# Attention and max-of-three feed-forward on one core: when batch 0 prepares its weights, and what the first steps load and wait for

## The chip, the core and the metric

The kernel runs on one core of a Trainium2 chip. The metric is the time of one execution in microseconds (us) on the device. Before the change it was run three times: 772.04, 774.18 and 776.42 us, median 774.18 us. A trace comes from one profiled execution more, of 775.52 us. In this document PE is the matrix engine (PEld its weight loads), DVE the vector engine, ACT the scalar engine, POOL the GpSimd engine, and SP the engine that issues most DMAs.

## The reference, cut to what matters

For 8 batches, 8 heads, 576 positions and head size 64:

```
rel    = i - j                                   (query minus key position)
scores = q k^T / 8 + slope_h * (-|rel|)          where 0 <= rel < 128, else -1e9
attn   = softmax(scores);  x = attn v            -> x is 4608 tokens x 512
h      = max(x w1, x w2, x w3)                   512 -> 768, elementwise maximum
out    = h w_out                                 768 -> 512
```

All in float32. Each query sees itself and at most 127 positions before it, so attention is done in bands of 128 queries.

## The kernel before

**Attention.** A task is one batch and one pair of heads (four tasks a batch). Two tasks give nine steps of 128 queries, so a batch has 18 steps (the name `n_steps`). Each two steps share one set of score matmuls (`products`, L381), then for each step come a masked copy and a fused add, scale and row minimum on DVE (`score`, L396, L399, L410), two exponentials on ACT (`exps`, L422), a reciprocal and the division (`sums_of`, `normalise`, L428 to L441), a transpose on PE with its copies (`turn`, L450 to L474) and the product with v (`mix` or `mix_rows`, L495 and L517).

**Feed-forward.** Products in nearly full float32 are made from two rounded pieces of each operand (hi and lo), and of 2x2 blocks with seven products instead of eight (a Strassen scheme). A weight group is 128 columns of w1, w2 or w3: nine groups, 0 to 8, and groups 9, 10 and 11 are the three parts of w_out. A unit is one of the seven products of one group for one batch: six matmuls of 128 by 288 (L707). A batch has 63 such units, and then 14 units that multiply by w_out.

**Weights.** They are prepared once, during batch 0. `preparing` (L270) is a generator that goes through the groups in the order `g_order` and does one of six parts each time that it is asked: the exponents, the conversion, parts 0 and 1 (round to hi on ACT, lo = source minus hi on DVE), part 2 and part 3 (sums of blocks on PE, then the same split). The first four groups of the order take a form with the exponents on DVE (L156, L165); the other eight have them on ACT (L158, L159, L169). A prepared group 0 to 8 lies in a ring of two places, is stored to DRAM for the later batches (`store`, L192), and its place is free for the group two later when the units that read it are done (`ahead`). If the next part has to wait for that, the generator stands still. The w_out groups have places of their own. The raw weights of a group come by DMA (`fetch`, L145) into one of two buffers.

**Who asks for parts.** `weights(n, upto)` adds n to an account and does one part for each whole one in it, and more if fewer than `upto` are done. Events are written out in order by `at(step, ...)` and sorted. Steps 5 to 19 ask for 1.6 parts each, and every unit of batch 0 for 1.3; in a unit `upto` is such that the parts that this unit multiplies by are done ahead of its matmuls in the program. Batch 0's units lie in the program between the steps of batch 1's attention. From the counters, the order puts these parts into these stretches:

```
parts of 72, in program order        steps 5-19   units 0-20   units 21-56
before (1.6 a step, 1.3 a unit)            25           19            28
groups begun in units 21-56: 5, 6, 7, 8 (each eight or nine units ahead of its first unit)
```

**Order of instructions.** The program order is the priority, and a scheduler at build time lets an engine take a later instruction where an earlier one isn't ready in its own model. An instruction given to `keep_in_program_order` stays where it is relative to its engine's others. Once built, each engine runs its list in order. `spin` (L325) puts bf16 matmuls of zeros on PE: seven at the start, and four after each second step of batch 0.

**The start.** SP issues q and k of task 0 (two DMAs), v of task 0, the identity, the raw weights of group 0, q and k of task 1, the raw weights of group 1, in this order. The score matmuls of steps 4 and 5 need q and k of task 1.

Of the kernel before, what the change touches and what calls it, by code (L numbers as in the profile page):

```python
# [26 lines left out]
RING = 2  # L27
SPIN, FIRST_SPIN = 4, 7

# [5 lines left out]
def attention_maxout_kernel(  # L35
# [117 lines left out]
    def exponents(g, few):  # L153
        _, t, top, small = pieces(g)
        if few:
            nc.vector.tensor_scalar(out=small, in0=top, scalar1=-56.0, scalar2=56.0, op0=ALU.max, op1=ALU.min)  # L156
        else:
            nc.scalar.activation(small, top, AF.Relu, bias=-56.0)  # L158
            nc.scalar.activation(t.bitcast(F32), top, AF.Relu, scale=-2.0 ** 27, bias=-56.0 * 2.0 ** 27)  # L159
# [107 lines left out]

    g_order = [0, 1, 9, 10, 11, 2, 3, 4, 5, 6, 7, 8]

# [93 lines left out]
    def products(s):  # L363
        whole = s < n_steps and s % 4 == 2
        ps = [ps_m.tile([P, 512], F32, name=f"ps_m{j}") for j in range(2)] if whole else [scores[:, j] for j in range(2)]
        for a, (t, i) in enumerate(steps[s:s + 2]):
            banks[s + a] = [x[:, a * 2 * P:(a + 1) * 2 * P] for x in ps], None if whole else a
            for j in range(2):
                for h in range(2):
# [16 lines left out]
                    ))  # L386

    def score(s):
        t, i = steps[s]
        b, hp = tasks[t]  # L390
        ps, a = banks.pop(s)
        if i:
            mask = prev[:, i == NB].bitcast(mybir.dt.uint8)
            if a is None:
                for x in ps:
                    nc.vector.copy_predicated(x[:, P:2 * P], mask, x[:, :P])  # L396
            else:
                both = scores[:, :, a * 2 * P:(a + 1) * 2 * P]
                nc.vector.copy_predicated(  # L399
                    both[:, :, P:], mask.unsqueeze(1).broadcast_to([P, 2, P]), both[:, :, :P],  # L400
                )

# [4 lines left out]
        for j in range(2):  # L407
            x = s_p.tile([P, P], F32, name="s", bufs=3)
            below = bias_t[:, hp // 2, j] if i == NB else (bias if i else bias0)[:, 2 * hp + j, :]
            nc.vector.tensor_tensor_reduce(  # L410
                out=x, in0=ps[j][:, P:2 * P], in1=below,
                scale=-0.125, scalar=3.0e38, op0=ALU.add, op1=ALU.min, accum_out=st[:, 0, s % 2, j:j + 1],
            )
            less[s].append(x)
# [256 lines left out]
    def unit(u):  # L671
# [14 lines left out]
        if g < 9:  # L686
            at = b * 9 + g
            if b == 0:
                weights(1.3, 6 * g_order.index(g) + 3 + (2, 2, 3, 3, 1, 2, 1)[k])
            x = xs[b, k]  # L690
# [86 lines left out]
    for s in range(5, n_steps + 2):  # L777
        at(s + 0.2, weights, 1.6)
        at(s + 0.7, rest)
# [9 lines left out]
    load(0)  # L789
    load_v(0)  # L790
    nc.sync.dma_start(dist[:, 2], c_ident)
    slopes(0)
    slopes_t(0)
    fetch(0)
    nc.scalar.copy(out=plus, in_=dist[:, 2])
    nc.scalar.activation(minus, dist[:, 2], AF.Copy, scale=-1.0)
    load(1)
    fetch(1)
# [40 lines left out]
```

## Time and profile before

| | |
|---|---|
| runs | 772.04, 774.18, 776.42 us |
| profiled execution | 775.52 us |
| its span, first to last instruction | 773.8 us |
| PE busy | 752.0 us (97%), weight loads 683.2 us (88%) |
| DVE, ACT, POOL busy | 546.6 (71%), 519.2 (67%), 193.5 us (25%) |
| mean granted PE clock | 0.991 of full speed |

Busy is the time in which an engine had at least one instruction in work. A row of a stage table gives the stretch, its length, busy time and instruction count (x) for each engine, the granted PE clock (1.00 is 2.4 GHz, 0.50 is 1.2 GHz), the share of the DMA engines and GB/s. A timeline row gives the start, the length, the engine, the line, the operation and its tiles, and in brackets the idle time of the engine just before and what ended it.

### The profile page before, as it was taken

What the parts mean: (1) busy time and instruction counts of PE and PEld (TensorE: products, weight loads), DVE (VectorE), ACT (ScalarE), POOL (GpSimd) and SP (SyncE); (2) the same over time, 40 slices, a digit from 0 to 9 for tenths busy, and PEclk for the clock granted to TensorE, in tenths of its full rate; (3) what the DMA queues carried; (4) which work ended last, traced back from release to release, by engine and by line L of the source; (5) the groups of instructions that cost most, each with busy time, mean ns of one, the idle gap of its engine ahead of it and who ended that gap; (6) DMA issues with size and microseconds to landing.
All of it is one profiled execution on the core that took longest, in us unless ns stands there. A gap on an engine that the chain in (4) does not pass through costs nothing.

```text
span 773.8 us, 19378 instructions
## 1 busy us (share of the span) xinstructions
PE 752.0 (97%) x7243; PEld 683.2 (88%) x7247; DVE 546.6 (71%) x1698; ACT 519.2 (67%) x1680; POOL 193.5 (25%) x403
## 2 busy tenths in 40 slices
PE   7898999999999999999999999999999999999998
PEld 2467787899999999999999999999999999999998
DVE  3878698986667947886677847785677847693673
ACT  5697889967668767677577766676676756652342
POOL 4350212311223222221232122221222122243100
PEclk8998999999999999999999999999999999999999
DMA  6674577783798649883788659983888558789721
GB/s 244 230 263 133 192 288 275 263 277 119 259 315 289 211 146 325 295 287 128 254 299 289 201 174 322 307 274 112 285 300 274 187 196 283 271 262 359 240 71 62
DMA packets 43838, 184.95 MB, mean 239 GB/s; under 512 B 4832, under 2 KB 14304, under 8 KB 34912
## 3 DMA queue, kind: packets, MB, share of 16 engines
q0 software_dynamic: 20304, 115.61, 45.1%
q1 hardware_dynamic: 23296, 67.97, 25.2%
q8 instruction: 57, 0.93, 0.5%
q14 instruction: 37, 0.30, 0.1%
q10 hardware_dynamic: 144, 0.13, 0.1%
HBM read 157.74 MB, written 25.95 MB: 237 GB/s over the span
## 4 chain that ended last, share of the span: by engine, by line
PE 67%; DVE 13%; ACT 7%; issue 1%; DVEq 0%; ACTq 0%
PE ps_m L707 54%; PE ps_s L381 4%; PE ps_x L517 4%; PE pt L450 3%; DVE hs L565 2%; ACT p L422 2%; DVE t L662 2%; DVE hq L663 2%; DVE t L568 1%; ACT t L723 1%; DVE xs L565 1%; PE pt L201 1%; ACT p L441 1%; ACT hs L564 1%; DVE xk L551 1%
## 5 line engine op out<-in xcount | busy, mean ns | idle before, releaser
L707 PE MATMUL ps_m<-xs,ring 128*128 128x288 f32 x2916 | 418.1, 298 | 2.9 <-ACT t L723 1.7
L707 PEld LDWEIGHTS ps_m<-xs,ring 128*128 128x128 f32 x2916 | 395.7, 189 | 10.1 <-ACT t L723 6.1
L723 ACT COPY t<-ps_m 128x288 f32<-128x288 f32 x262 | 102.8, 394 | 79.3 <-PE ps_m L707 77.0
L707 PE MATMUL ps_m<-hs,ow 128*128 128x288 f32 x1008 | 141.6, 297 | 1.1 <-DVE hs L565 0.4
L707 PEld LDWEIGHTS ps_m<-hs,ow 128*128 128x128 f32 x1008 | 134.6, 188 | 4.6 <-ACT t L723 1.9
L422 ACT ACTIVATE p<-s,st 128x128 f32<-128x128 f32 x288 | 115.2, 403 | 13.8 <-DVE st L410 12.8
L470 POOL TENSOR_SCALAR_AFFINE_SELECT pp<-pr 128x256 f32<-128x256 f32 x112 | 51.1, 456 | 289.4 <-ACT pr L454 167.1
L317 POOL DMA_DIRECT2D ring<-keep x121 | 65.1, 538 | 202.4 <-PE ps_m L707 195.4
L441 ACT ACTIVATE p<-p,st 128x128 f32<-128x128 f32 x252 | 86.0, 396 | 26.8 <-DVE st L429 26.8
L662 DVE TENSOR_TENSOR t<-ps_m,t 128x288 f32<-128x288 f32 x144 | 65.0, 453 | 50.3 <-PE ps_m L707 34.8
L410 DVE CUSTOM_DVE_ANT_0 s<-ps_s,bias 128x128 f32<-128x128 f32 x240 | 61.0, 286 | 9.9 <-POOL bias_t L109 3.9
L663 DVE TENSOR_TENSOR hq<-t,hq 128x288 f32<-128x288 f32 x144 | 65.8, 463 | 2.5
L381 PE MATMUL ps_s<-qk 64*64 64x192 f32 (+1 forms) x1088 | 63.4, 317 | 2.9 <-DMA qk<-in_qk 2.5
L517 PE MATMUL ps_x<-pp,v 64*64 64x64 f32 (+3 forms) x1456 | 56.2, 274 | 0.0
L422 ACT ACTIVATION_READ_ACCUMULATOR p<-s,st 128x1 f32 x288 | 56.0, 194 | 0.0
L564 ACT CAST hs<-hq 128x288 fp32r<-128x288 f32 x96 | 40.1, 434 | 22.7 <-DVE hq L663 19.3
L551 DVE TENSOR_TENSOR xk<-ps_x,xk 128x256 f32<-128x256 f32 (+3 forms) x56 | 25.5, 456 | 39.0 <-ACT xk L550 39.0
L517 PEld LDWEIGHTS ps_x<-pp,v 64*64 64x64 f32 x1456 | 42.9, 133 | 11.1 <-issue 9.8
L474 POOL TENSOR_SCALAR_AFFINE_SELECT pp<-pr 128x256 f32<-128x256 f32 (+1 forms) x112 | 50.1, 447 | 1.1
L450 PE MATMUL pt<-plus,p 128*128 128x128 f32 x288 | 48.6, 289 | 1.3 <-POOL p L436 0.6
L450 PEld LDWEIGHTS pt<-plus,p 128*128 128x128 f32 x288 | 30.5, 141 | 20.5 <-issue 15.1
L381 PEld LDWEIGHTS ps_s<-qk 64*64 64x64 f32 x1088 | 40.0, 134 | 9.5 <-issue 3.9
(123 smaller groups left out, 829.3 us busy)
## 6 DMA issues: line engine op xcount, KB each, us to landing
ring<-keep POOLq DMA_DIRECT2D x60, 1024.0 KB, 7.4
ring<-keep POOLq DMA_DIRECT2D x61, 768.0 KB, 5.8
qk<-in_qk SPq DMA_DIRECT2D x31, 576.0 KB, 5.6
hs<-in_w_all SPq DMA_DIRECT2D x12, 1023.6 KB, 5.8
v<-in_v SPq DMA_DIRECT2D x32, 320.0 KB, 5.7
keep<-ring SPq DMA_DIRECT2D x9, 1024.0 KB, 5.5
outT<-t SPq DMA_DIRECT2D x64, 144.0 KB, 1.8
keep<-ring SPq DMA_DIRECT2D x9, 768.0 KB, 4.9
```

What stands on the lines that cost most here:

```text
L317: nc.gpsimd.dma_start(wts[n, a], keep[n % 9][a])
L381: pe(nc.tensor.matmul(ps[j][d:d + D, o:o + k1 - k0], lhsT=qkt[u][j * D:(j + 1) * D, 0, q0:q0 + D], rhs=qkt[u][j * D:(j + 1) * D, 1, k0:k1] ...
L410: nc.vector.tensor_tensor_reduce(out=x, in0=ps[j][:, P:2 * P], in1=below, scale=-0.125, scalar=3.0e38, op0=ALU.add, op1=ALU.min, accum_out ...
L422: nc.scalar.activation(p[:, j], x, AF.Exp, bias=st[:, 0, a, j:j + 1], scale=-1.0, accum_out=st[:, 1, a, j:j + 1])
L441: nc.scalar.activation(p[:, j], p[:, j], AF.Copy, scale=st[:, 2, a, j:j + 1])
L450: pe(nc.tensor.transpose(out=pt[:, a, j], in_=p[:, j], identity=ident))
L470: nc.gpsimd.affine_select(out=old, in_=src, pattern=[[-x, n] for x, n in pat], compare_op=ALU.is_gt, fill=0.0, base=0, channel_multiplier=1,)
L517: pe(nc.tensor.matmul(x[j * D:(j + 1) * D, r, o:o + rhs.shape[1]], lhsT=vv[k, i, j * D:(j + 1) * D], rhs=rhs[k], start=start, stop=True, s ...
L662: nc.vector.tensor_tensor(out=s, in0=ps, in1=e, op=ALU.add)
L663: nc.vector.tensor_tensor(out=h, in0=s, in1=h, op=ALU.max)
L707: pe(nc.tensor.matmul(part_of[n, {2: 0, 5: 0, 6: 0, 3: 1}.get(kk, kk)], lhsT=lt, rhs=rt, start=first, stop=i == len(pairs) - 1, skip_group ...
L723: nc.scalar.copy(out=e, in_=ps)
```

## The change

Four edits. (1) Batch 0's steps ask for 0.7 parts instead of 1.6, and its units for 1.0 instead of 1.3. (2) The order of the groups becomes 0, 1, 2, 9, 3, 4, 10, 5, 6, 11, 7, 8. (3) At the start, q and k of task 1 are issued ahead of the raw weights of group 0, v of task 0 behind them, and five spins are done instead of seven. (4) DVE's instructions of the scores of steps 0 to 5, and the exponents of groups 0 and 1, keep their program order.

```diff
-SPIN, FIRST_SPIN = 4, 7
+SPIN, FIRST_SPIN = 4, 5
+FIRST = 6
...
-            nc.vector.tensor_scalar(out=small, in0=top, scalar1=-56.0, scalar2=56.0, op0=ALU.max, op1=ALU.min)
+            x = nc.vector.tensor_scalar(out=small, in0=top, scalar1=-56.0, scalar2=56.0, op0=ALU.max, op1=ALU.min)
+            if g < 2:
+                tc.keep_in_program_order(x)
...
-    g_order = [0, 1, 9, 10, 11, 2, 3, 4, 5, 6, 7, 8]
+    g_order = [0, 1, 2, 9, 3, 4, 10, 5, 6, 11, 7, 8]
...
+    def dve(s, ins):
+        if s < FIRST:
+            tc.keep_in_program_order(ins)
...
-                    nc.vector.copy_predicated(x[:, P:2 * P], mask, x[:, :P])
+                    dve(s, nc.vector.copy_predicated(x[:, P:2 * P], mask, x[:, :P]))
...
-            nc.vector.tensor_tensor_reduce(
+            dve(s, nc.vector.tensor_tensor_reduce(
...
-                weights(1.3, 6 * g_order.index(g) + 3 + (2, 2, 3, 3, 1, 2, 1)[k])
+                weights(1.0, 6 * g_order.index(g) + 3 + (2, 2, 3, 3, 1, 2, 1)[k])
...
-        at(s + 0.2, weights, 1.6)
+        at(s + 0.2, weights, 0.7)
...
     load(0)
-    load_v(0)
     nc.sync.dma_start(dist[:, 2], c_ident)
     slopes(0)
     slopes_t(0)
+    load(1)
     fetch(0)
+    load_v(0)
     nc.scalar.copy(out=plus, in_=dist[:, 2])
     nc.scalar.activation(minus, dist[:, 2], AF.Copy, scale=-1.0)
-    load(1)
     fetch(1)
```

With it the counters give:

```
parts of 72, in program order        steps 5-19   units 0-20   units 21-56
after (0.7 a step, 1.0 a unit)             10           16            46
groups 3, 5 and 7: parts 0, 1 and 2 all stand in the program at their own first
unit (21, 35, 49), just ahead of its matmuls; for 5 and 7 the exponents and the
conversion stand there too. For 4, 6 and 8, part 2 stands one unit ahead of the
first unit and part 3 at it. Before, part 3 of groups 3 to 8 stood two or three
units ahead of the group's first unit.
```

## Rows read from the trace of the kernel before

**Rows 1.** The profile's first part: busy time of each engine over the whole span.

```profile
PE 752.0 (97%) x7243; PEld 683.2 (88%) x7247; DVE 546.6 (71%) x1698; ACT 519.2 (67%) x1680; POOL 193.5 (25%) x403
```

**Rows 2.** The table by stage: first steps, the rest of batch 0's attention, units 0 to 20, units 21 to 56; then two finer stretches from another such table, the second of them in the later batches.

```profile
0.00:20.00 20.00, 14.38 (x89) 5.63 (x90) 8.07 (x39) 10.54 (x44) 9.04 (x24) 0.83 0.66 236
20.00:63.00 43.00, 39.90 (x309) 23.79 (x311) 32.87 (x103) 35.10 (x107) 19.08 (x33) 1.00 0.70 248
63.00:103.00 40.00, 35.44 (x241) 29.68 (x239) 31.25 (x76) 30.93 (x78) 5.71 (x8) 0.91 0.51 186
103.00:160.00 57.00, 54.03 (x533) 46.98 (x532) 50.11 (x133) 49.81 (x144) 15.03 (x27) 1.00 0.71 255
...
100.00:120.00 20.00, 19.49 (x192) 15.98 (x194) 17.80 (x54) 19.36 (x56) 5.53 (x11) 1.00 0.71 255
...
220.00:240.00 20.00, 20.00 (x247) 18.62 (x246) 14.87 (x50) 14.04 (x48) 6.59 (x14) 1.00 0.90 299
```

**Rows 3.** The timeline of the first 13 us, in part: the issue of the raw weights and of q and k of task 1, DVE's first score and its first weight instruction, the first two and the other fourteen score matmuls of steps 4 and 5.

```profile
3.27 0.43 SPq L145 DMA_DIRECT2D hs<-in_w_all  x1
3.75 0.44 SPq L344 DMA_DIRECT2D qk<-in_qk  x1
...
6.34 0.29 DVE L410 CUSTOM_DVE_ANT_0 s<-ps_s,bias 128x128 f32<-128x128 f32 x1 [3.94 <-POOL bias_t L109]
...
9.53 0.54 PE L381 MATMUL ps_s<-qk 64*64 64x192 f32 x2 [0.40 <-DVE st L410]
...
11.19 0.69 DVE L156 TENSOR_SCALAR hs<-hs 128x1024 int8<-128x1024 int8 x1 [1.51 <-DMA hs<-in_w_all]
...
12.61 1.34 PE L381 MATMUL ps_s<-qk 64*64 64x192 f32 x14 [2.55 <-DMA qk<-in_qk]
```

**Rows 4.** The table by stage around that wait (columns as in rows 2), and a DVE row of the timeline in its last stretch.

```profile
10.00:12.60 2.60, 0.06 (x1) 0.00 (x0) 1.41 (x7) 1.12 (x8) 0.14 (x1) 0.88 0.85 357
12.60:18.60 6.00, 5.77 (x31) 2.49 (x32) 3.01 (x15) 3.72 (x18) 1.83 (x4) 0.50 0.46 164
...
19.64 0.30 DVE L396 COPY_PREDICATED ps_m<-prev,ps_m 128x128 f32<-128x128 uint8 x1 [1.92 <-PE ps_m L381]
```

**Rows 5.** The timeline of ACT: the first exponential of step 0, of step 5 and of step 17.

```profile
6.92 0.39 ACT L422 ACTIVATE p<-s,st 128x128 f32<-128x128 f32 x1
...
18.25 0.39 ACT L422 ACTIVATE p<-s,st 128x128 f32<-128x128 f32 x1
...
54.54 0.39 ACT L422 ACTIVATE p<-s,st 128x128 f32<-128x128 f32 x1
```

**Rows 6.** The groups of instructions by line from 103 to 160 us (busy us, mean ns of one, idle before): the weight preparation. Behind them, from the same view of the first 110 us, two of the form that the first four groups take; and the busy time on PE in 103 to 160 us of L201 alone and of L187 alone.

```profile
L197 DVE TENSOR_TENSOR ring<-hs,ring 128x512 fp32r<-128x512 f32 x10 | 7.5, 746 | 0.9 <-ACT ring L196 0.9
L196 ACT CAST ring<-hs 128x512 fp32r<-128x512 f32 x10 | 6.8, 679 | 0.6 <-DVE hs L172 0.6
...
L169 DVE SCALAR_TENSOR_TENSOR hs<-hs 128x1024 int32<-128x1024 int8 x4 | 5.1, 1268 | 0.5 <-ACT hs L159 0.4
L172 DVE SCALAR_TENSOR_TENSOR hs<-hs 128x1024 uint32<-128x1024 uint32 x4 | 4.9, 1218 | 0.0
...
L159 ACT ACTIVATE hs<-hs 128x1024 f32<-128x1024 int8 x4 | 4.7, 1174 | 0.0
...
L158 ACT ACTIVATE hs<-hs 128x1024 int8<-128x1024 int8 x3 | 3.5, 1158 | 0.0
L197 DVE TENSOR_TENSOR ring<-pt,ring 128x512 fp32r<-128x512 f32 x5 | 3.4, 685 | 1.5 <-ACT ring L196 1.5
...
L188 ACT CAST ring<-pt 128x512 fp32r<-128x512 f32 x5 | 2.9, 589 | 1.3 <-PE pt L187 1.2
L196 ACT CAST ring<-pt 128x512 fp32r<-128x512 f32 x5 | 2.9, 587 | 1.0 <-PE pt L201 1.0
L222 ACT CAST ring<-pt 128x512 fp32r<-128x512 f32 x5 | 2.9, 585 | 3.6 <-PE pt L201 2.2 <-DVE ps_s L399 1.4
...
L165 DVE CUSTOM_DVE_ANT_0 hs<-hs 128x1024 int32<-128x1024 int8 x4 | 4.9, 1221 | 0.0
...
L156 DVE TENSOR_SCALAR hs<-hs 128x1024 int8<-128x1024 int8 x4 | 3.0, 752 | 1.5 <-DMA hs<-in_w_all 1.5
...
103.00:160.00 57.00, 11.79 (x70) 9.17 (x70) 1.00 0.71 255
...
103.00:160.00 57.00, 2.49 (x5) 0.93 (x5) 1.00 0.71 255
```

**Rows 7.** The timeline of PE where batch 0's units begin, and the granted clock by the table of single microseconds (columns as in rows 2).

```profile
66.24 0.47 PE L201 MATMUL pt<-ow,plus 128*128 128x256 f32 x2 [2.11 <-DVE ow L197]
67.29 5.65 PE L707 MATMUL ps_m<-xs,ring 128*128 128x288 f32 x22 [0.57 <-DVE xs L565]
...
67.00:68.00 1.00, 0.71 (x3) 0.71 (x4) 1.00 (x3) 1.00 (x3) 0.00 (x0) 0.50 0.00 0
```

**Rows 8.** The timeline: ACT's first exponent instruction of group 5 and the copy that ends unit 21 (group 5's exponents stand in the program at unit 27).

```profile
100.48 1.14 ACT L158 ACTIVATE hs<-hs 128x1024 int8<-128x1024 int8 x1
...
103.54 0.39 ACT L723 COPY t<-ps_m 128x288 f32<-128x288 f32 x1
```

**Rows 9.** The timeline of POOL: the first load of a stored group for batch 1.

```profile
156.29 0.75 POOL L317 DMA_DIRECT2D ring<-keep  x1 [1.55 <-PE ps_m L707]
```

More of the change, by code (lines that the diff above doesn't have):

```diff
@@ L395, in score @@
                 for x in ps:
-                    nc.vector.copy_predicated(x[:, P:2 * P], mask, x[:, :P])
+                    dve(s, nc.vector.copy_predicated(x[:, P:2 * P], mask, x[:, :P]))
             else:
                 both = scores[:, :, a * 2 * P:(a + 1) * 2 * P]
-                nc.vector.copy_predicated(
+                dve(s, nc.vector.copy_predicated(
                     both[:, :, P:], mask.unsqueeze(1).broadcast_to([P, 2, P]), both[:, :, :P],
-                )
+                ))
         if s % 2 == 0:
@@ L409, in score @@
             below = bias_t[:, hp // 2, j] if i == NB else (bias if i else bias0)[:, 2 * hp + j, :]
-            nc.vector.tensor_tensor_reduce(
+            dve(s, nc.vector.tensor_tensor_reduce(
                 out=x, in0=ps[j][:, P:2 * P], in1=below,
                 scale=-0.125, scalar=3.0e38, op0=ALU.add, op1=ALU.min, accum_out=st[:, 0, s % 2, j:j + 1],
-            )
+            ))
             less[s].append(x)
```

## The prediction, made before the changed kernel was run

> **What bounds the kernel now.** I read the share of each engine first [rows 1]: PE has work in 97% of the span. The reader then has to see that this average hides two regimes. In the later batches PE is full (20.00 of 20 us) and DVE and ACT have room; nothing of the change touches that code. In the first 160 us no engine is full [rows 2]: from 20 to 63 us (batch 0's attention from step 6) PE is busy 39.9 of 43, ACT 35.1, DVE 32.9; from 63 to 103 us (units 0 to 20) 35.4, 30.9 and 31.3 of 40; from 103 to 160 us (units 21 to 56) 54.0, 49.8 and 50.1 of 57. All of this is start-up: the same weight preparation has to be fitted somewhere, and the later batches can't start before it is through. So the question is what it costs in the stretch that it leaves and in the one that it enters. I call the stretches A (0 to 20), B (20 to 63), C1 (63 to 103) and C2 (103 to 160).
>
> **A, the order of the first loads and the pinned DVE.** Two waits stand in A [rows 3]. PE does two matmuls of steps 4 and 5 at 9.53 us and the other fourteen at 12.61, 2.55 us idle for q and k of task 1, whose DMA was issued at 3.75, behind the raw weights (issued at 3.27). DVE stands 1.51 us at the head of its queue with group 0's exponents, whose weights come at 11.19; queued behind them are the scores of steps 2 and 3 and the reciprocal that the first division waits for. The change issues q and k of task 1 first and holds the exponents behind the scores of step 5, so both waits go. The second price hangs on the first: after the pause the granted clock is 0.50 for 6 us [rows 4], PE is busy in 5.77 of these, and at 19.64 DVE has waited 1.92 us for it. Over the pause itself it was 0.88 on average, so it fell at the pause's end. At full speed most of those 1.92 us go too.
>
> The DMA wait alone is 2.55 us; with 1.92 us of the slow stretch and 1.51 us of DVE's wait, were they all in one chain, 6.0. The two first overlap partly, so A gives 2.5 to 6.5 us (the upper end with up to half a microsecond of the two spins, which would otherwise be hidden: the first score starts at 6.34, when POOL's bias work ended [rows 3]). I take 5, near the upper end, because pause and slow clock stand one behind the other. What is late next is the chain of exponentials and divisions on ACT. v of task 0 is issued behind 1 MB more, and its first use comes only at 20 us; that is hidden, and so is the later landing of group 0's weights, which are not asked for before step 6. The pin adds a wait: a score that waits for PE holds back all that is behind it on DVE, at most the 1.9 us of one such wait, which the ends hold.
>
> **The price of a part** [rows 6]. One group with the exponents on ACT costs ACT 1.16 + 1.17 (exponents), 2 x 0.68 (parts 0, 1), 0.59 (part 2) and 0.59 + 0.59 (part 3), 5.45 us; DVE 1.27 + 1.22 (conversion), 2 x 0.75 and 0.69, 4.7 us; PE (11.79 + 2.49) / 5 = 2.86 us. With the exponents on DVE, as the first four groups of either order have them, ACT pays 3.1 and DVE 0.75 + 1.22 + 1.22 + 2.2 = 5.4 us.
>
> **B, fifteen parts fewer.** The steps lose groups 9 and 10, parts 2 and 3 of group 1 and the exponents of 11: ACT 2 x 3.1 + 1.76 + 2.33 = 10.3 us, DVE 2 x 5.4 + 0.7 = 11.4, PE 3 x 2.86 = 8.6. By ACT at its present density (82%) B would shrink by 10.3 / 0.82 = 12.6; by PE at its density (93%) by 8.6 / 0.93 = 9.2. A lower end comes from the pace of the steps [rows 5]: steps 5 to 17 take 36.3 us, 3.02 a step with 1.6 parts each; steps 0 to 5, without parts but with A's waits, 2.27. That is at least 0.47 us a part, so 0.9 parts less in twelve steps give 5.1 us. I take 8, near PE's row, since PE is what is fullest there.
>
> **C1, three parts fewer.** Here ACT loses exponents (groups 2 and 9 now take the DVE form): before, 3 x 3.1 + 3 x 2.33 = 16.3 us; after, 1.8 + 2 x 3.1 + 2.33 = 10.3. DVE loses 2.6, PE nothing. C1 is held by the burst that splits batch 0's attention result into seven factors, with PE idle for 2.11 us behind a subtraction of group 11 and then at a clock of 0.50 [rows 7]. Group 11 is gone from there, but the exponents and conversion of group 2 come in on DVE. From 0 to 4 us; I take 2, the row's own wait.
>
> **C2, eighteen parts more, three groups.** ACT gets 3 x 5.45 = 16.4, DVE 14, PE 8.6 us. ACT then has 49.8 + 16.4 = 66.2 us of work. One group's exponents (2.33) will be done ahead in C1, as group 5's are now, which start 3 us before unit 21 ends although they stand at unit 27 [rows 8]. ACT has reached 19.36 of 20 us in one stretch, 97% [rows 2]; at that, 63.9 / 0.97 = 66 us for C2. PE gives the same: (54.0 + 8.6) / 0.948 = 66. So C2 grows from 57 to 66, by 9. The ends: two groups' exponents ahead and ACT without a gap, 61.5 us, +4.5; ACT at its present density of 87%, 66.2 / 0.874 = 75.7, +18.7.
>
> Behind unit 56 nothing changes: the last part falls at unit 56 instead of 54, and the first reload for batch 1 (now at 156.3 us [rows 9]) has the 14 units of w_out as cover; cost nothing, some 2 us if those were gone.
>
> **The sum.** -5 - 8 - 2 + 9 = -6 us. It is made on the profiled execution, 775.5 us, and gives 769.5; that execution stands 1.3 us above the median of the runs shown, so 768 us on their scale.
>
> A page bears on the direction of all this. PE's busy share in C2 is 95%, its weight loads' 82% [rows 2]. The Trainium skill (Perfetto Trace Analysis, section Identifying the Most-Contended Engine) judges TensorE's headroom by the weight loads and not by matmul time; by that rule PE leaves room and ACT alone sets C2, by the row itself PE would set it, and the sum is the same to a microsecond. The same page (section Optimization Strategy) says that regimes with different limits may gain from being interleaved; here that speaks against taking weight work out of the attention, whose ACT has 18% to spare, into C2, whose ACT has 13%, and it is the second rival below that works this out.
>
> **The rivals.**
> *C2 absorbs the parts (764 or less, taken as 761).* C2 +4.5 and B -11: -5 - 11 - 2 + 4.5 = -13.5, 775.5 - 13.5 - 1.3 = 761. For it: the first 160 us have all engines at 80 to 90%. Against: ACT would need no gaps for 61 us, and the densest stretch is 97%.
>
> *Only moved (773).* C2 stays at its density, +18.7, against -5 - 8 - 2 or a little more: the attention's gain is given back, and A's gain is eaten by the denser stretch. About +3 to -4 us, 773 as its middle. For it: the total of ACT and PE work is the same before and after. Against: B and C1 have their own idle time, which the parts didn't all fill.
>
> *Weights too late (780, slower).* The place is units 21, 35 and 49, the first of groups 3, 5 and 7. There parts 0 to 2 stand directly ahead of the matmuls that use them, and everything of PE's list is queued behind: later units, the scores and transposes of batch 1. The chain at such a unit is exponents 2.33, conversion 2.49, one cast and subtraction 0.68 + 0.75, part 2 on PE 1.6 (8 of 14 matmuls of 2.86), 0.59 + 0.69: 9.1 us. With exponents and conversion pulled ahead 4.3 us remain. A set of scores is some 1 us of other work (fourteen of its matmuls took 1.34 at the low clock [rows 3]), so a stall is 3 to 8 us, three times 9 to 24. With the middle of the lower half, three times 4, it comes to 768 + 12 = 780. It decides from (778 - 768) / 3 = 3.4 us a place. For it: at 66.24 PE stood 2.11 us for just such a subtraction, 22 feed-forward matmuls behind it [rows 7]. Against: exponents do run ahead [rows 8], and the ring place is free since unit 16, 30 or 44. The Trainium skill (TensorE: Matmul & The Clock Gate, section Step-by-step: what each phase is for) says that matmuls stay in program order and only weight loads are pulled ahead; the 2.11 us agree with it, and by it alone each such wait is paid in full.
>
> *The change doesn't do what it says.* If q and k of task 1 still came late, A would give nothing: 773, inside the second rival's time.
>
> **Chances.** Forecast (763 to 773, its middle 768) 0.48; absorbed 0.15; only moved 0.18; too late 0.19. What a measurement of this kernel can tell from no change is about 0.5%, 3.9 us: faster is below 770.3, slower above 778.05. Of the forecast about 70% lie below 770.3 (0.335) and 30% above (0.145). Faster: 0.335 + 0.15 + 0.02 of only moved, 0.505; same: 0.145 + 0.13, 0.275; slower: 0.19 + 0.03, 0.22. The summed ends, -6.5 - 12.6 - 4 + 4.5 and -2.5 - 5.1 + 18.7, give -18.6 and +11.1; they won't all fall together, and with the third rival's lower half in it the range is 759 to 780.
>
> **What would show it.** Right if in the new trace the fourteen matmuls of steps 4 and 5 follow the first two without a DMA wait, the clock stays at 1.00 from 10 to 20 us, step 5's first exponential comes 4 to 6 us before 18.25, step 17's some 13 us before 54.54, and unit 21 some 15 us before 103.5. Then the stretch from unit 21 to the end of unit 56 should take 66 us, with ACT above 95%. Wrong if PE shows waits of over 3 us for a subtraction of groups 3, 5 or 7; if ACT in C2 stays at 87%; or if the steps' pace stays near 3 us with fewer parts, since then a chain of latencies and not the parts set it.

## The result, and the profile after

The changed kernel takes 779.89 us (median of 6 executions, 778.0 to 782.48), the kernel before beside it on the same chip 772.83: ratio 1.0085, with a 95% interval of 1.0065 to 1.0105. It is slower; the forecast was faster by 0.8%. 779.89 lies just inside the range of 759 to 780 and on the time of the rival "weights too late". Three executions far off the others, two of e9's four (the profiled one among them) at 1432 us and one of e2's ten at 1466, are left out of every median and ratio below, so that e9's median is of two and it has no marks.

The first part of the profile after, and its table by stage in the windows of [rows 2]. The profiled execution took 780.24 us, its span 778.5.

```profile
PE 754.6 (97%) x7245; PEld 684.1 (88%) x7245; DVE 545.4 (70%) x1698; ACT 519.5 (67%) x1680; POOL 195.3 (25%) x403
```

```profile
0.00:20.00 20.00, 15.46 (x117) 6.52 (x117) 11.44 (x52) 13.01 (x55) 12.47 (x29) 1.00 0.73 267
20.00:63.00 43.00, 37.75 (x297) 23.07 (x298) 29.23 (x93) 32.89 (x105) 19.21 (x30) 0.92 0.51 175
63.00:103.00 40.00, 38.18 (x323) 31.60 (x321) 33.55 (x91) 31.89 (x89) 7.12 (x12) 1.00 0.67 244
103.00:160.00 57.00, 50.18 (x412) 41.03 (x413) 44.71 (x114) 46.59 (x116) 9.29 (x18) 0.94 0.61 228
```

The whole-span shares are those of before [rows 1]. The stages are not: from 103 to 160 us PE is busy 50.18 us for 54.03 and its granted clock 0.94 for 1.00 [rows 2]. The slow clock of the first stage (0.83) is gone, and a new one stands in the second (0.92).

To see where time is won and lost I set marks in both traces: the first exponential of a step, and ACT's copy that closes the first unit of a group (L730 after, L723 before). Of after, ACT's timeline at step 17, at units 21 and 56, and at unit 63, where batch 0's units of w_out begin:

```profile
49.93 0.43 ACT L429 ACTIVATE p<-s,st 128x128 f32<-128x128 f32 x1
...
90.08 0.41 ACT L730 COPY t<-ps_m 128x288 f32<-128x288 f32 x1
...
163.72 0.40 ACT L730 COPY t<-ps_m 128x288 f32<-128x288 f32 x1 [0.82 <-PE ps_m L714]
...
175.19 0.39 ACT L730 COPY t<-ps_m 128x288 f32<-128x288 f32 x1
```

In before, step 17 comes at 54.54 [rows 5], unit 21 at 103.54 [rows 8], unit 56 at 159.70 and unit 63 at 170.53. The change is 4.3 us ahead at step 5 (13.98 for 18.25), 4.6 at step 17, 13.5 at unit 21, and 4.0 behind at unit 56, 4.7 at unit 63. From unit 63 to the end both spans need 603.3 us (778.5 - 175.19 and 773.8 - 170.53). All that the change does to the time is done by then, and it is lost between units 21 and 56: 73.6 us for 56.2. The stretches that lose are those that end with units 21, 35 and 49: from the unit seven before, they take 17.8, 19.7 and 21.6 us for 11.8, 13.0 and 11.4. The table by stage over these three stretches of after, columns as in [rows 2]:

```profile
72.25:90.08 17.83, 16.09 (x140) 13.15 (x140) 14.77 (x41) 15.51 (x42) 5.64 (x9) 1.00 0.60 226
101.75:121.47 19.72, 16.52 (x122) 13.30 (x122) 15.85 (x42) 15.81 (x44) 3.95 (x7) 0.92 0.62 228
133.67:155.31 21.64, 18.49 (x169) 15.23 (x167) 18.61 (x48) 18.30 (x49) 2.93 (x6) 0.94 0.52 193
```

No engine is full in them, and PE is idle for 1.7, 3.2 and 3.2 us; over the same three stretches of before it is idle for 1.8 in all. So the engines wait for one another there, and none lacks capacity. At unit 49 a single row says so. The timeline of PE at this unit:

```profile
148.06 0.77 PE L384 MATMUL ps_s<-qk 64*64 64x128 f32 x14
151.44 0.40 PE L714 MATMUL ps_m<-xs,ring 128*128 128x288 f32 x1 [2.61 <-ACT ring L199]
152.00 0.40 PE L714 MATMUL ps_m<-xs,ring 128*128 128x288 f32 x1 [0.16 <-ACT ring L199]
```

and of ACT:

```profile
149.73 1.11 ACT L161 ACTIVATE hs<-hs 128x1024 int8<-128x1024 int8 x1 [0.56 <-DMA hs<-in_w_all]
150.75 1.19 ACT L199 CAST ring<-hs 128x512 fp32r<-128x512 f32 x2
151.84 1.18 ACT L162 ACTIVATE hs<-hs 128x1024 f32<-128x1024 int8 x1
```

PE stands 2.61 us for the casts of group 7 (L199), parts 0 and 1 of the group that unit 49 is about to use. ACT has in front of them the exponents of the next group, 8 (L161), whose raw weights had just landed. The clock is then 0.50 for 3.4 us, until about 156 us (the row 153 to 155 us has 0.50, 155 to 157 has 0.76). A second stretch of 3.4 us at 0.50 begins at 118.4 us, ahead of unit 35, behind PE waits of 0.59, 0.67 and 1.00 us for parts of group 10.

### The profile page after: what moved, and what is told of

Same layout as the page of the kernel before. It is cut to its first block, busy times and chain, and to the rows that moved or that the text cites. A ratio compares the mean times of both kernels' runs of the same rounds, so it can differ in the third digit from the quotient of the medians.

```text
span 778.5 us, 19396 instructions
## 1 busy us (share of the span) xinstructions
PE 754.6 (97%) x7245; PEld 684.1 (88%) x7245; DVE 545.4 (70%) x1698; ACT 519.5 (67%) x1680; POOL 195.3 (25%) x403
## 4 chain that ended last, share of the span: by engine, by line
PE 75%; DVE 12%; ACT 8%; DMA 2%; issue 1%; POOL 1%; SPq 0%; DVEq 0%; ACTq 0%; POOLq 0%
PE ps_m L714 57%; PE ps_s L384 4%; PE pt L457 4%; PE ps_x L524 4%; DVE hs L572 2%; ACT p L429 2%; PE pt L204 2%; DVE hq L670 2%; DVE t L669 2%; DVE t L575 1%; PE ps_x L502 1%; DMA hs<-in_w_all 1%; ACT p L448 1%; ACT t L730 1%; PE ps_m L384 1%
## 5 line engine op out<-in xcount | busy, mean ns | idle before, releaser
L730 ACT COPY t<-ps_m 128x288 f32<-128x288 f32 x262 | 102.7, 393 | 81.6 <-PE ps_m L714 79.1
L477 POOL TENSOR_SCALAR_AFFINE_SELECT pp<-pr 128x256 f32<-128x256 f32 x112 | 55.0, 491 | 289.2 <-ACT pr L461 159.5
L429 ACT ACTIVATE p<-s,st 128x128 f32<-128x128 f32 x288 | 115.1, 403 | 13.6 <-DVE st L417 11.0
L524 PE MATMUL ps_x<-pp,v 64*64 64x64 f32 (+3 forms) x1456 | 59.2, 275 | 1.1 <-POOL pp L477 1.1
L524 PEld LDWEIGHTS ps_x<-pp,v 64*64 64x64 f32 x1456 | 43.7, 133 | 13.9 <-issue 10.6
L406 DVE COPY_PREDICATED ps_s<-prev,ps_s 128x256 f32<-128x256 uint8 x105 | 44.5, 424 | 4.7 <-PE ps_s L384 3.2
```

The source lines that it names most:

```text
L429: nc.scalar.activation(p[:, j], x, AF.Exp, bias=st[:, 0, a, j:j + 1], scale=-1.0, accum_out=st[:, 1, a, j:j + 1])
L477: nc.gpsimd.affine_select(out=old, in_=src, pattern=[[-x, n] for x, n in pat], compare_op=ALU.is_gt, fill=0.0, base=0, channel_multiplier=1,)
L524: pe(nc.tensor.matmul(x[j * D:(j + 1) * D, r, o:o + rhs.shape[1]], lhsT=vv[k, i, j * D:(j + 1) * D], rhs=rhs[k], start=start, stop=True, s ...
L730: nc.scalar.copy(out=e, in_=ps)
```

## The experiments

One table has all the runs; the edits, expectations and readings follow it. Medians in us; ratio to the kernel before on the same chip with its 95% interval ("one run" is one execution, which has no interval and stands on its own); the marks are of the profiled execution.

| run | median | ratio | step 5 | step 17 | unit 21 | unit 49 | unit 63 |
|---|---|---|---|---|---|---|---|
| before | 772.83 | 1 | 18.25 | 54.54 | 103.54 | 150.13 | 170.53 |
| after | 779.89 | 1.0085 (1.0065 to 1.0105) | 13.98 | 49.93 | 90.08 | 155.31 | 175.19 |
| e1 start edits only | 778.55 | 1.0065 (1.0047 to 1.0084) | 13.98 | 54.49 | 100.20 | 148.08 | 170.02 |
| e2 weight edits only | 777.39 | 1.0053 (1.0032 to 1.0073) | 17.95 | 52.14 | 86.64 | 152.83 | 172.03 |
| e3 after, 2.0 a unit | 774.43 | 1.0020 (1.0003 to 1.0037) | 14.03 | 47.07 | 84.58 | 146.59 | 169.42 |
| e4 after, 1.6 a step, 1.3 a unit | 778.32 | 1.0057 (1.0036 to 1.0079) | 14.00 | 55.19 | 92.02 | 148.91 | 170.03 |
| e5 loads only | 773.95 | 1.0007 (0.9993 to 1.0022) | 17.31 | 54.54 | 102.52 | 149.06 | 169.47 |
| e6 pins only | 781.21 | 1.0114 (1.0043 to 1.0184) | 16.48 | 56.95 | 102.64 | 151.94 | 173.87 |
| e7 e2 with 2.0 a unit | 772.13 | 0.9987 (0.9966 to 1.0007) | 17.02 | 51.19 | 88.14 | 144.23 | 167.12 |
| e8 e3, no parts in steps | 783.64 | one run | 14.46 | 39.77 | 97.12 | 156.03 | 178.84 |
| e9 after, no pins | 778.70 | 1.0086 (1.0055 to 1.0116) | - | - | - | - | - |
| e10 e3, no pins | 777.44 | 1.0063 (1.0033 to 1.0094) | 19.14 | 57.40 | 94.81 | 152.05 | 175.56 |
| e11 pinned scores only | 777.90 | one run | 20.80 | 58.59 | 106.16 | 152.71 | 173.10 |
| e12 pinned exponents only | 778.03 | one run | 16.48 | 56.24 | 102.72 | 151.08 | 172.99 |
| e13 five spins only | 778.68 | 1.0070 (1.0055 to 1.0085) | 19.56 | 57.16 | 104.01 | 151.92 | 173.81 |
| e14 e1 with seven spins | 775.91 | one run | 13.95 | 53.78 | 99.44 | 149.18 | 171.06 |
| e15 e3 with seven spins | 775.77 | 1.0033 (1.0020 to 1.0046) | 14.84 | 50.71 | 87.07 | 148.27 | 171.11 |
| e16 after, exponents on DVE | 777.75 | 1.0043 (1.0022 to 1.0065) | 14.07 | 49.84 | 87.95 | 151.97 | 171.80 |
| e17 e7, exponents on DVE | 770.85 | 0.9961 (0.9939 to 0.9984) | 16.01 | 49.63 | 85.22 | 139.77 | 162.97 |
| e18 before, exponents on DVE | 771.37 | 0.9978 (0.9962 to 0.9994) | 15.95 | 53.41 | 98.11 | 146.98 | 167.21 |

### The change in halves

e1 keeps the start (loads, pins, five spins) and undoes the weights, e2 the reverse. e3 and e4 are the whole change with other rates:

```diff
 e3
-                weights(1.0, 6 * g_order.index(g) + 3 + ...
+                weights(2.0, 6 * g_order.index(g) + 3 + ...
 e4
-                weights(1.0, 6 * g_order.index(g) + 3 + ...
+                weights(1.3, 6 * g_order.index(g) + 3 + ...
-        at(s + 0.2, weights, 0.7)
+        at(s + 0.2, weights, 1.6)
```

> The first loads, the spins and the pinned DVE order of the change alone; parts and group order as before. If the gain of stretch A (step 5's first exponential 4.3 us earlier in the changed kernel) reaches the end: 768 to 769 us against 772.8 before. If the rest of batch 0's attention gives it back, as its pace in the changed kernel suggests: 772 to 773.

> 0.7 parts a step, 1.0 a unit and the new group order alone; the start as before. If the start edits are worth 4 us: 784. If they are worth nothing: 780. Below 776 would mean that the start edits do the harm.

> The changed kernel with 2.0 parts a unit instead of 1.0: parts 0 to 2 of groups 3, 5 and 7 then stand 3 to 6 units ahead of the group's first unit instead of at it; as many parts leave the steps as in the change. Theory 'too late' (the parts stand directly ahead of their use): the loss of units 14 to 56 goes, 769 or less. Rival 'too much work' (46 parts in units 21 to 56, whatever their place): part of the load moves to units 0 to 20, but the total is the same, 777 to 780.

> The changed kernel with the rates of before (1.6 a step, 1.3 a unit) and the new group order. The ring stops the steps at 14 parts, and parts 0 to 2 of groups 3, 5 and 7 stand one to three units ahead. 'Too late': about 771 to 774, between the changed kernel and one with more lead. 'Too much work': 777 to 780, since 43 parts stay in units 21 to 56.

Each half alone is slower. e1 shows the head start of 4.3 us at step 5 and nothing of it at step 17. e2 loses its lead between units 21 and 49, as the whole change does. With twice the parts a unit the ratio falls by 0.65% on either start: from 1.0085 (after) to 1.0020 (e3), and from 1.0053 (e2) to 0.9987 (e7, below). So the slow rate is worth most of the change's loss. e3's 774.43 us lies between its two forecasts, 769 or less and 777 to 780. In its profile unit 63 comes 5.8 us sooner. The three stretches before units 21, 35 and 49 shrink from 59.2 us to 40.7, the other stretches from unit 14 to unit 63 grow by 11.9. The rows of the table by stage before unit 21, where PE's idle time falls from 1.7 to 0.7 us, and before unit 49, from 3.2 to 0.4 at a clock that is low all the same, and then the row of the whole stretch from unit 21 to unit 56:

```profile
73.04:84.58 11.54, 10.88 (x86) 9.02 (x88) 7.68 (x19) 8.40 (x23) 1.84 (x4) 1.00 0.75 266
...
133.09:146.59 13.50, 13.13 (x104) 10.97 (x103) 11.12 (x28) 11.83 (x27) 1.66 (x4) 0.87 0.47 166
...
84.58:158.41 73.83, 67.00 (x583) 55.14 (x583) 63.43 (x151) 63.94 (x166) 15.46 (x29) 0.98 0.70 258
```

The last row matters: in e3 units 21 to 56 take 73.8 us, as long as in after (73.6), and what its profile wins is won ahead of unit 21. With the old start the same stretch does shrink, from 74.6 us in e2 to 66.7 in e7. Their rows, e2 first:

```profile
86.64:161.21 74.57, 68.61 (x601) 56.08 (x601) 60.95 (x161) 64.31 (x172) 12.73 (x28) 0.98 0.64 233
...
88.14:154.80 66.66, 61.49 (x571) 51.13 (x569) 58.41 (x147) 59.55 (x161) 14.96 (x28) 1.00 0.72 255
```

The faster rate also does two things at once. By the counters it makes parts 0 to 2 of groups 3, 5 and 7 four to six units ahead of their first unit, and it leaves 39 parts in units 21 to 56 where the change has 46. e4 has 43 there, one to three units ahead. By its ratio (1.0057, 778.32 us) it falls under "too much work"; in its profiled execution, 775.14 us and so one of its faster ones, the stretch takes 67.0 us. No run keeps the number of parts and moves only their place, so how much of the 0.65% is lateness and how much is the number of parts stays open.

### The start edits apart, and the pace of the steps

```diff
 e5, on the kernel before
-    load_v(0)
+    load(1)
     fetch(0)
+    load_v(0)
 e6, on the kernel before: the pins alone (FIRST = 6, exponents of groups 0 and 1)
 e7, on e2
-                weights(1.0, ...
+                weights(2.0, ...
 e8, on e3
-        at(s + 0.2, weights, 0.7)
+        at(s + 0.2, weights, 0.0)
```

> The kernel before with the order of the first loads alone changed (q and k of task 1 ahead of the raw weights, v of task 0 behind them); seven first spins, nothing pinned, old weights. Theory P (the pins hold VectorE's queue and cost the start edits their gain): the loads alone keep the gain, first exponential of step 5 near 14 us and of step 17 1 to 4 us before 54.5, time 3 to 5 us under the kernel before, ratio 0.994 to 0.996. Rival L (what is won at the head is lost again by step 17 whatever the pins do, since the weight parts then run beside GpSimd's selections and divisions): step 5 near 14, step 17 within 1 us of 54.5, ratio 1.000 to 1.006.

> The kernel before with the pins alone (scores of steps 0 to 5 and the exponents of groups 0 and 1 in program order on VectorE); old loads, seven first spins, old weights. Theory P: slower, ratio 1.004 to 1.008, with the first exponential of step 17 later than 54.5. Rival L: no change, ratio 0.999 to 1.002, step 17 within 1 us of 54.5.

> The kernel before with the new order of groups, 0.7 parts a step and 2.0 parts a unit; the old start. If the costs are separate terms (late weights some 5.5 us, the start edits some 5), this run has neither: 3 to 5 us under the kernel before, ratio 0.993 to 0.997, and the first copies of units 35 and 49 no later than in the run of 2.0 parts a unit with the new start. If the two runs with half the change each paid for one and the same thing (lost time in batch 0 that any denser stretch brings), it comes out at 774 again, ratio 1.000 to 1.003.

> The changed kernel with 2.0 parts a unit and no weight parts in the steps of batch 0's attention at all (they move into the units). If the parts set the pace of steps 5 to 17, these twelve steps take some 25 us for the 36 of the changed kernel. If the attention's own chain sets it (scores, exponentials, division, transposes), they take 30 us or more. The whole is expected slower than the changed kernel with 2.0 a unit, 776 to 784 us, since units 7 to 49 wait for their parts.

The loads alone do nothing: DVE still stands for group 0's exponents, and step 5 gains 0.9 us. The pins alone gain 1.8 us at step 5, are 2.4 behind at step 17, and cost 0.4 to 1.8%. Together they gain 4.3 at step 5, more than the 2.7 of both apart: this fits a DMA wait and a wait of DVE that lie partly side by side, so that either one, left in, hides part of what removing the other gives. e7 has neither of the two harms and is level with the kernel before; against e3 the new start costs some 0.3%, where the two intervals still overlap a little.

Why the pins harm shows at 33 us. With them group 0's exponents start at 16.16 us instead of 11.19, the weight work behind them moves too, and conversions on DVE now run beside POOL's selections. POOL's timeline of the kernel before at the first four selections of that round:

```profile
33.96 0.41 POOL L470 TENSOR_SCALAR_AFFINE_SELECT pp<-pr 128x256 f32<-128x256 f32 x1 [6.15 <-ACT pr L454]
34.31 0.41 POOL L474 TENSOR_SCALAR_AFFINE_SELECT pp<-pr 128x256 f32<-128x256 f32 x1
34.68 0.41 POOL L470 TENSOR_SCALAR_AFFINE_SELECT pp<-pr 128x256 f32<-128x256 f32 x1
35.04 0.86 POOL L474 TENSOR_SCALAR_AFFINE_SELECT pp<-pr 128x256 f32<-128x256 f32 x1
```

and of e6, the same four, with the conversions on DVE's timeline behind them:

```profile
33.24 1.11 POOL L477 TENSOR_SCALAR_AFFINE_SELECT pp<-pr 128x256 f32<-128x256 f32 x1 [6.50 <-ACT pr L461]
34.31 1.39 POOL L481 TENSOR_SCALAR_AFFINE_SELECT pp<-pr 128x256 f32<-128x256 f32 x1
35.66 0.40 POOL L477 TENSOR_SCALAR_AFFINE_SELECT pp<-pr 128x256 f32<-128x256 f32 x1
36.02 1.39 POOL L481 TENSOR_SCALAR_AFFINE_SELECT pp<-pr 128x256 f32<-128x256 f32 x1
```

```profile
32.87 1.22 DVE L168 CUSTOM_DVE_ANT_0 hs<-hs 128x1024 int32<-128x1024 int8 x1
...
34.21 1.22 DVE L175 SCALAR_TENSOR_TENSOR hs<-hs 128x1024 uint32<-128x1024 uint32 x1
...
35.68 1.46 DVE L168 CUSTOM_DVE_ANT_0 hs<-hs 128x1024 int32<-128x1024 int8 x1
```

Each selection that starts under a conversion lasts until 0.26 or 0.27 us behind that conversion's end. The other way round, the conversion at 35.68 started beside a selection already under way and took 1.46 us for 1.22. From 13 to 64 us PE waits for POOL for 5.1 us in e6; in before it is 1.1 (0.6 and 0.5). The view of waits of e6 in this stretch:

```profile
PE ps_x L502 <- POOL pp L477: 2.8, 4, 1.1
PE pt L457 <- POOL p L443: 2.3, 3, 1.3
```

e8 settles the pace. Without parts the twelve steps from 5 to 17 take 25.3 us, 2.11 a step, as expected of parts and not of a chain of latencies. With 0.7 a step they take 36.0 after and 33.0 in e3, with 1.6 a step 36.3 before and 40.5 in e1. No single price of a part comes out of this, since the last of these steps hold other work too. With fewer parts in the steps the first units move up among them; PE's first unit matmuls in after, then in before:

```profile
44.47 1.03 PE L714 MATMUL ps_m<-xs,ring 128*128 128x288 f32 x6
...
51.66 0.67 PE L707 MATMUL ps_m<-xs,ring 128*128 128x288 f32 x3
```

Up to the first exponential of step 17, PE has done twelve unit matmuls in after and five in before.

### The pins, and the spins

e9 and e10 are after and e3 with nothing pinned, e11 and e12 the kernel before with one kind of pin each, e13 the kernel before with the spins alone, e14 and e15 are e1 and e3 with seven spins.

```diff
 e9, e10 (e12 has the first line alone, e11 the second, both on e6)
-FIRST = 6
+FIRST = 0
-            if g < 2:
+            if g < 0:
 e13, on the kernel before
-SPIN, FIRST_SPIN = 4, 7
+SPIN, FIRST_SPIN = 4, 5
```

> The whole change with nothing pinned on VectorE. If the pins are what the start edits cost (theory P), the ratio to the kernel before falls from 1.0085 to 1.004 to 1.006: only the late weights are left, the first copies of units 35 and 49 still coming late (over 118 and 150 us). First exponential of step 5 near 17.3, as with the loads alone. If the loss is the same whatever the start (rival L), 1.007 to 1.010 again.

> The change with 2.0 parts a unit and nothing pinned: new loads, five first spins, new order, 0.7 a step. By theory P with the terms separate it stands at the run of 2.0 a unit with the old start, ratio 0.997 to 1.000, first step 5 near 17.3 and units 35 and 49 near 116 and 144 us. If the loads or the two spins harm in this company, 1.002 as with the pins.

> The kernel before with only the scores of steps 0 to 5 pinned, the exponents free. Theory: what harms is that the pinned exponents of group 0 leave VectorE's gap at 11 to 16 us and then run, with their conversion, beside GpSimd's selections and divisions; then this run goes as the kernel before, step 17's first exponential within 1 us of 54.5. Rival: the pinned scores harm, step 17 near 57.

> The kernel before with only the exponents of groups 0 and 1 pinned. Theory (the exponents' pin harms): exponents of group 0 at 15 us or later for 11.2, step 17's first exponential 1.5 to 3 us later than 54.5. Rival (the pinned scores harm): step 17 within 1 us of 54.5.

> The kernel before with five first spins for seven and nothing else. If the two spins less are what every slower start has in common (theory S), the first exponential of step 0 comes later than 7 us by 2 or 3, as in the two runs without pins, and the ratio is 1.003 to 1.006. If the spins are hidden behind GpSimd's bias work, as the prediction had it, 0.999 to 1.001.

> The start edits alone (new order of the loads, all the pins) with the old weights and seven first spins. By theory S the first exponentials of steps 12 and 17 come 2 to 4 us sooner than with five spins (39.8 and 54.5) and the time is 770 to 773. If the arrangement of VectorE's weight work is what harms, they stay within 1 us of 39.8 and 54.5, and the time near 775 to 779.

> The change with 2.0 parts a unit and seven first spins. By theory S it comes under the run with the old start (ratio 0.9987), at 0.995 to 0.998. Otherwise it stays at the 1.002 of the same kernel with five.

The theory that the pins are the loss of the start fell with e9 and e10: without them the change is no faster, and with 2.0 parts a unit slower by 0.4%. e11 and e12 don't name one pin either, each alone is late at step 17. e13 shows what the pins are good for. Two spins fewer cost 0.7% by themselves, which the prediction had as hidden. DVE's timeline of e13 begins so:

```profile
8.68 0.29 DVE L396 COPY_PREDICATED ps_m<-prev,ps_m 128x128 f32<-128x128 uint8 x1 [6.28 <-PE ps_m L381]
8.89 0.28 DVE L410 CUSTOM_DVE_ANT_0 s<-ps_s,bias 128x128 f32<-128x128 f32 x1
```

In before, DVE's first attention work is step 0's score, at 6.34 [rows 3]. With five spins, in the program as written out, step 2's masked copy stands ahead of it, waits 6.28 us for matmuls of PE, and step 0's first exponential comes at 9.22 for 6.92. The spins' own time is hidden: after has five too, with the pins, and its step 0 comes at 6.82. What differs at the start of e13 is the order of the instructions that comes with the number of spins. That this order is the whole of the 0.7% was not shown. The pins hold that order, and with pins five spins cost nothing against seven (e15 is no faster than e3, and at step 17 e14 is 0.7 us ahead of e1).

### The exponents

```diff
 e16, on after; e17, on e7; e18, on the kernel before
-FEW = 4
+FEW = 12
```

> The changed kernel with the exponents of all twelve groups on VectorE for four of them. If ScalarE's queue is what makes the parts late at units 21, 35 and 49 (the exponents of the next group stand ahead of the casts that a unit waits for), the 2.6 us of TensorE's wait at unit 49 goes, the stretch from unit 21 to unit 56 gets 3 to 6 us shorter than 73.6, and the ratio falls from 1.0085 to 1.001 to 1.005. If it is the landing of the raw weights or the order of the parts itself, the wait moves to VectorE's conversion, the stretch stays within 2 us and the ratio stays at 1.006 or more.

> The kernel before with the new order of groups, 0.7 parts a step, 2.0 parts a unit, and the exponents of all twelve groups on VectorE; the old start. In the changed kernel the exponents on VectorE gave back some 3 us. If that is worth the same where the parts are no longer late, the ratio is 0.993 to 0.997 and this is faster than both kernels. If it only cured the late parts, which 2.0 a unit cures already, it stays at the 0.9987 of the run without, 0.996 to 1.001.

> The kernel before with the exponents of all twelve groups on VectorE and nothing else. If ScalarE's exponents were a cost of the kernel before too, the ratio is 0.994 to 0.998. If they hurt only where the parts are made right ahead of their matmuls, it is 0.999 to 1.002, or slower by as much as VectorE's own waits grow.

e16 gives back 0.4%, a ratio within the first forecast's range, but not in the way expected. Units 21 to 56 take 73.0 us for 73.6, and 2.1 of the 3.4 us that its profile wins at unit 63 are won ahead of unit 21. Unit 49 still waits, now for the conversion that DVE ends at 146.9 us. PE's timeline of e16:

```profile
147.64 1.18 PE L714 MATMUL ps_m<-xs,ring 128*128 128x288 f32 x2 [2.30 <-ACT ring L199]
```

So ACT's queue was only the last link. The wait there is for the chain itself, made right ahead of the unit. e18 shows that the exponents on ACT were a cost of the kernel before as well, 0.2%; e17 has the same edit on e7, whose own 0.1% is within its interval, and is the fastest of all, 770.85 us, 0.4% under the kernel before and 1.2% under the change. Its row from unit 21 to unit 56, and the same of after:

```profile
85.22:150.23 65.01, 64.31 (x580) 53.26 (x578) 60.41 (x151) 50.12 (x149) 18.17 (x28) 1.00 0.77 274
```

```profile
90.08:163.72 73.64, 66.73 (x553) 54.73 (x548) 58.04 (x150) 60.46 (x160) 11.67 (x24) 0.95 0.67 247
```

PE has 0.7 us of idle time in the first and 6.9 in the second, and the clock of the first is 1.00. The stretch takes 65 us, a microsecond less than the prediction gave C2, with 39 parts in it for the change's 46.

## Why the prediction was wrong

**A, -5: right in kind and size, and not kept.** The fourteen matmuls follow the first two without a DMA wait. PE's timeline of after:

```profile
8.86 0.77 PE L384 MATMUL ps_s<-qk 64*64 64x192 f32 x16
```

The clock is 1.00 to 20 us, and step 5 comes 4.3 us sooner. That the pin adds a wait was seen; that it moves the weight work to another time was not. After step 5 the exponents and conversions stand beside POOL. The timeline of after, of DVE, of POOL, then of PE:

```profile
16.71 0.79 DVE L157 TENSOR_SCALAR hs<-hs 128x1024 int8<-128x1024 int8 x1
17.53 1.31 DVE L168 CUSTOM_DVE_ANT_0 hs<-hs 128x1024 int32<-128x1024 int8 x1
...
19.22 1.32 DVE L175 SCALAR_TENSOR_TENSOR hs<-hs 128x1024 uint32<-128x1024 uint32 x1
```

```profile
16.55 0.41 POOL L477 TENSOR_SCALAR_AFFINE_SELECT pp<-pr 128x256 f32<-128x256 f32 x1 [2.51 <-ACT pr L461]
16.91 0.86 POOL L481 TENSOR_SCALAR_AFFINE_SELECT pp<-pr 128x256 f32<-128x256 f32 x1
17.73 1.38 POOL L477 TENSOR_SCALAR_AFFINE_SELECT pp<-pr 128x256 f32<-128x256 f32 x1
...
19.44 2.14 POOL L443 TENSOR_TENSOR p<-p,st 128x256 f32<-128x256 f32 x2
```

```profile
21.07 1.01 PE L457 MATMUL pt<-plus,p 128*128 128x128 f32 x4 [2.24 <-POOL p L443]
```

The table by stage of after in the next microseconds:

```profile
22.00:24.00 2.00, 2.00 (x12) 0.91 (x12) 0.66 (x2) 1.89 (x8) 1.23 (x3) 0.71 0.01 4
24.00:26.00 2.00, 2.00 (x8) 0.60 (x6) 0.27 (x3) 1.44 (x7) 0.53 (x1) 0.50 0.00 0
26.00:28.00 2.00, 2.00 (x22) 1.36 (x18) 0.00 (x0) 0.64 (x1) 0.00 (x0) 0.50 0.20 37
```

PE idles 2.24 us, and the clock is at its lower level (0.50, 1.2 GHz) for 6.8 us of 20 to 30 us. The pause and the slow clock that A takes away from 10 to 19 us stand here again, 10 us later. The pause comes with the kernel, the slow clock need not: e3 differs only in what the units ask for, its PE has the same pause, and its clock stays at 1.00. The timeline of PE in e3, and its table by stage:

```profile
21.12 1.01 PE L457 MATMUL pt<-plus,p 128*128 128x128 f32 x4 [2.25 <-POOL p L443]
...
22.00:24.00 2.00, 2.00 (x15) 0.99 (x14) 0.60 (x1) 1.83 (x7) 1.17 (x3) 1.00 0.02 4
24.00:26.00 2.00, 2.00 (x27) 1.14 (x25) 0.53 (x4) 2.00 (x9) 0.58 (x1) 1.00 0.00 0
```

Step 12's first exponential comes at 30.94 us in e3 and at 33.78 in after.

**B, -8 by step 17: won by step 12, and not there at step 17.** The twelve steps take 36.0 us for 36.3. But the seven from step 5 to step 12 take 22.7 us before, 19.8 in after (with the slow clock), 16.9 in e3, 16.3 in e2, and 14.8 in e8 without parts. So fewer parts do quicken the steps, by 5.7 us in e3. The five steps from 12 to 17 then take 16.2 us in after and 16.1 in e3 for 13.6: the units that move up stand there, and POOL's selections take 0.82 us each for 0.65 before. How much is units and how much collisions was not separated. The term had neither. The pace of 3.0 us a step was named as a sign of being wrong, for a chain of latencies; e8 shows that it is not that.

**The sum up to unit 21, -15: right by its total.** It was -13.5, since the units started sooner than forecast: from step 17 to unit 14 they took 22.3 us for 37.2. What B did not show at step 17 came free there.

**C2, +9: the step that failed.** The forecast put 62.6 us of PE work (54.0 + 8.6) into 66 us: it let PE and ACT run at 95 to 97% and at full clock, with parts that stand right ahead of their use. From unit 21 to unit 56 the kernel before takes 56.2 us, with PE busy in 53.2; the changed one takes 73.6, with PE busy in 66.7. Of these +17.5 us, 8.6 are the PE work that was forecast. About 3.4 are slow clock: two stretches of 3.4 us at the lower level, 6.8 us, of which half is lost if PE is full in them. Some 1.5 are other PE work, and 3.9 are idle time of PE, 6.9 us for 3.0. So the work was sized to 1.5 us, and the density and the clock were not. ACT was to be above 95%; it is at 82% (60.46 of 73.64). The mean share of a stretch was taken for what an order of work can reach whose parts stand at their own unit. What the runs show in its place: PE stands 2.61 us at unit 49 for parts of its own group (1.97 in e2, 2.30 in e16), e3, e7 and e17 have no such wait, and asking for the parts twice as fast is worth 0.65%. That lateness alone makes C2 long is not shown, since e3's C2 takes 73.8 us without that wait. With +17.5 for +9 the sum is +2.5; the rest of the profile's +4.7 is 1.5 us less lead at unit 21 and 0.7 after unit 56.

**The rival "weights too late"** named the units, the parts and the direction. The faster rate takes back 0.65% of the time, as it would have it, but by fewer parts as well as by earlier ones, so that the runs support it and do not prove it. Its price was a stall of 4 us at each of three places. The trace has one of 2.61 us; the rest of the loss is smaller idle pieces, slow clock and work. So that its time of 780 came out is partly luck. "C2 absorbs" asked for a dense stretch, and e17 shows one, at 2.0 parts a unit and with the exponents off ACT.

**The rest.** The half microsecond that the two spins might give had the wrong sign wherever nothing was pinned (e13). C1's -2 can't be told apart from B. Behind unit 56 nothing changes, as forecast: 0.7 us to unit 63, and 603.3 us in both from there. "Only moved" had C2's size nearly right (+18.7 for +17.5), but from ACT at its old density of 87%, where 82% was measured, and it gave the attention's stretch more lead to pay with. "The change doesn't do what it says" fell with step 5.

**What stays open.** Whether the parts of the change cost because they come late or because there are more of them in units 21 to 56, as said above. And e1 reaches unit 63 0.5 us before the kernel before in its profile and takes 5 us longer by the medians; its ten executions lie from 774.48 to 779.71 at clocks of 0.995 to 0.988, the profiled one (775.05) near the fast end. The clock alone is not it: three of them at 0.993 took 775.05, 777.25 and 778.84. e4, with the same start and the same 1.6 parts a step, is alike (unit 63 at 170.03, median 778.32). What the slower executions wait for was not seen, as only one is profiled.

## What to carry to other kernels

Price a moved piece of work by what stands beside it in its new place, and not by its mean: here a weight conversion on VectorE stretched a GpSimd selection that started under it from 0.4 to as much as 1.4 us. When preparation is moved into the stretch that uses it, ask how many units ahead it is made and how much of it is left in that stretch; the share of busy time tells only that there is room, and here doubling the rate was worth 0.65%. A mark at which a gain is to be seen has to lie ahead of the work that moves up behind it, as step 12 did here and step 17 did not. And an edit of the head that looks free (two warm-up matmuls) is measured alone too, since it can change the order of instructions on an engine that it does not touch.

## What the hardware showed that I had not expected

A selection on POOL takes 0.41 us alone and 1.38 to 1.39 under a conversion on DVE that reads two tensors of SBUF (the rows at 17.73 us after, 34.31 in e6). The Trainium skill (SBUF — State Buffer, section SBUF: two separate sides) says that the two engines share a pair of ports by an exclusive lock, also for a DVE operation with two SBUF inputs against a GpSimd one that reads SBUF, and that the other blocks for the whole instruction. The rows agree: a selection ends 0.27 us behind the conversion that it started under. The selections at 16.91 us after and at 35.04 before do the same behind exponents (16.71 to 17.50 and 34.78 to 35.63), which read one tensor; so two inputs are not needed for it. The prediction, which weighed engines one by one, had no term for it.

The time of e17 goes with the clock of the execution: its eleven lie between 766.51 us at a mean granted clock of 1.000 and 774.74 at 0.991, 13.9 us at the lower level (0.009 x 2 x 774). Slow stretches came behind waits of PE of 2.55 us [rows 3], 2.11 [rows 7], 2.24 and 2.61 (above), and lasted 6.8 us behind the 2.24 and 3.4 behind the 2.61. But the same wait in the same place, 2.25 us in e3, had none behind it. So a wait that is removed in one place and comes back in another can bring a slow stretch along, and one profile does not tell whether it always does.
